# A sketched attention with a squared-ReLU feed-forward on one core: the order of the first weight loads, and the row length of one weight

## The chip, the cores and the metric

One core of a Trainium2 chip runs the whole kernel. The metric is the device time of one execution in microseconds, the median of several. The core's engines work side by side, each through its own queue of instructions in order: TensorE (PE, with the weight loads shown as PEld), VectorE (DVE), ScalarE (ACT), GpSimd (POOL) and SyncE (SP), which here issues nearly all DMA transfers.

## What is computed

Four batches with four heads, 1,088 positions and a head width of 32. q and k are sketched to 64 features, attention is linear in them, and its output, laid out as 4,352 rows of 128, goes through a feed-forward with a hidden width of 2,048. All data are float32.

```python
def phi(x):
    a = np.einsum('rd,bhsd->bhsr', S1, x)          # r = 8
    b = np.einsum('rd,bhsd->bhsr', S2, x)
    return np.einsum('bhsi,bhsj->bhsij', a, b).reshape(*x.shape[:-1], r * r)
q_p, k_p = (phi(q), phi(k))
kv = np.einsum('bhsf,bhsd->bhfd', k_p, v)
z = np.sum(k_p, axis=2)
num = np.einsum('bhsf,bhfd->bhsd', q_p, kv)
den = np.einsum('bhsf,bhf->bhs', q_p, z)[..., None] + 1e-06
x = (num / den).transpose(0, 2, 1, 3).reshape(4352, 128)
h = np.maximum(x @ w_in, 0.0)                      # w_in 128 x 2048
out = h * h @ w_out                                # w_out 2048 x 128
```

## The kernel before

The attention output is kept transposed in SBUF as `xT` (128 x 4,352). The feed-forward runs over ten blocks of its columns (`FC`: 256, 384, 448, 448, 512 five times, 256). For each block it walks through 16 slices of 128 hidden units: `ffn1` (L582) multiplies a slice of `w_in` with the block into PSUM tile `pg`, `relu` (L591, on ACT) takes it to `gt`, `square` (L599 on ACT or L601 on DVE) to `g`, and `ffn2` (L620) adds `w_o` slice times `g` to the output tile `po`. Slices are grouped into units of up to 512 columns: in the first block, unit 0 and 1 hold one slice each and units 2 to 8 two each. PE runs the first products of up to four units ahead of the second products.

Start-up is written out by hand. SP issues its loads in one list: k and the first 256 columns of q for batch 0, eight loads of v, then the ten loads that the change permutes: four quarters of `w_in`, four of `w_o`, and the second and third part of q. `load_wi` (L204) brings a quarter of 512 columns, 128 rows of 2,048 bytes, into `w_in32`. `load_wo` (L209) brings 512 rows of `w_out`; partition p receives the four rows 4p to 4p + 3 of the quarter, which lie together in memory as 2,048 bytes. Hidden unit 4p + j of a quarter thus sits in partition p of slice j. To match this, `cast_wi` (L664, on POOL) rounds a quarter of `w_in32` to the matmul's float32r type and gathers every fourth column, so that slice j holds the hidden units 4i + j.

The first 256 columns of `xT` come from a special short path that ends at L810. What follows in each engine's queue is fixed in advance by a list scheduler (`_Order`), which works with constant estimates of the durations; the engines then wait for one another through semaphores. Around the change these steps stand in this order:

- POOL: the four casts, then 16 small copies (L496) that spread the reciprocal of the denominator (`rc`) into `rd`.
- DVE: `xT` (L810); two transposes of q's second part into `qT` (L288); the squares of units 0 and 1 (L601); `qt` (L468); `pd` (L474), a product of two SBUF operands; a sum (L484) and the reciprocal `rc` (L488); the shuffles `qb`, `qa` (L505) and products `qp` (L520); `bc` (L545), which waits for POOL's copies; and `xT` for the next 384 columns (L552); then the transposes of the next k (L276).
- PE: `ffn1` of units 0, 1 and 2; the sketch of q's second part, `qc` (L295); then `ffn1` and `ffn2` in turn; `nd` (L535), which needs `qp`; `ffn1` of unit 8; and `ffn1` of the second block, which needs the `xT` of L552.

Unit 3 is the first to read the second quarter of the weights, unit 5 the third, unit 7 the fourth. After the ten loads SP issues k, v and q of batch 1, and then output stores (L634) and the loads of later batches as their buffers come free. Each DMA also waits, on SP, for the landing of the one eight places before it.

Of the kernel before, what the change touches and what calls it, by code (L numbers as in the profile page):

```python
# [14 lines left out]
def _ap(t: bass.AP, p0: int, np_: int, off: int, free):  # L15
    p = list(t.ap)[0]
    return bass.AP(
        t.tensor, t.offset + p0 * p[0] + off, [[p[0], np_]] + [list(d) for d in free]
    )
# [85 lines left out]
def kernel(  # L105
# [11 lines left out]
    nc = tc.nc  # L117
# [38 lines left out]
    def sb(name, cols, dt=F32, rows=128):  # L156
        return cpool.tile([rows, cols], dt, tag=name, name=name)
# [9 lines left out]
    w_in32, w_o, w_in = sb("w_in32", 2048), sb("w_o", 2048), sb("w_in", 2048, F32R)  # L167
# [14 lines left out]
    def load_q(eng, b, c0, c1):  # L182
        eng.dma_start(  # L183
            qn[b % 2][:, c0:c1],
            bass.AP(q.tensor, q.offset + b * H * S * D + c0, [[G * D, 128], [1, c1 - c0]]),
        )
# [16 lines left out]
    def load_wi(eng, c):  # L203
        eng.dma_start(  # L204
            w_in32[:, 512 * c : 512 * c + 512], moe_w_in[:, 512 * c : 512 * c + 512]
        )

    def load_wo(eng, c):
        eng.dma_start(  # L209
            w_o[:, 512 * c : 512 * c + 512],  # L210
            bass.AP(
                moe_w_out.tensor, moe_w_out.offset + c * 512 * 128, [[512, 128], [1, 512]]
            ),
        )

# [446 lines left out]

    def cast_wi(c):
        nc.gpsimd.tensor_copy(  # L664
            _ap(w_in, 0, 128, 512 * c, [[128, 4], [1, 128]]),
            _ap(w_in32, 0, 128, 512 * c, [[1, 4], [4, 128]]),
        )

    def keep_warm(n, cols=512):
# [15 lines left out]
        )  # L685
    nc.scalar.copy(ss[:, :], sp[:, 0:80])
    load_wi(nc.sync, 0)
    load_wo(nc.sync, 0)
    load_q(nc.sync, 0, 256, 640)
    for c in range(1, 4):  # L690
        load_wi(nc.sync, c)
        load_wo(nc.sync, c)
    load_q(nc.sync, 0, 640, S)
    keep_warm(W1)
# [76 lines left out]
    for c in range(4):  # L771
        cast_wi(c)
# [308 lines left out]
```

## Time and profile before

| | us |
|---|---|
| median of 3 runs (lowest, highest) | 187.6 (186.36, 187.63) |
| the profiled execution's own time | 187.6 |
| its span, from the first to the last instruction | 185.5 |

The span leaves out 2.1 us around the program. The page gives the busy time of each engine, 40 slices of the span with the busy tenths of each engine, the chain of work that ended last (followed back from the last instruction to whatever released it), and groups of equal instructions. Three rows of the 40 slices:

```profile
PE   8988899999999999999999999999999999999992
...
POOL 4446504418400000770000003830000000000000
...
DMA  4789900100028700000591100002103000300111
```

A slice is 4.6 us; 9 means 90% or more. The DMA row is the mean busy share of the core's 16 DMA engines. The loads concerned and their landing, from issue, as medians of each kind:

```profile
w_in<-in_moe_w_in_dram SPq DMA_DIRECT2D x4, 256.0 KB, 4.8
w_o<-in_moe_w_out_dram SPq DMA_DIRECT2D x4, 256.0 KB, 4.9
```

### The profile page before, as it was taken

The page shows a single profiled execution, that of the slowest core. Times are in us where ns is not written, and L with a number is a line of the kernel's source. Part 1 is how long each engine was busy: PE and PEld are TensorE (multiplying, and loading weights), DVE is VectorE, ACT ScalarE, POOL GpSimd, SP SyncE. Part 2 cuts the span into 40 slices and gives each one's busy share as a digit, 9 for nine tenths or more (in the row PEclk, how much of TensorE's full clock was granted, in tenths as well). Part 3 has the DMA queues.
Part 4 walks back from the last instruction along what each step waited for, and adds up shares of the span by engine and source line. Part 5 has one row for each costly group of instructions (what it writes and reads, how often), then busy time and mean ns, then how long its engine had stood idle before and what let it go on. Part 6 is the DMA issues. An engine that isn't in the chain of part 4 may idle for free.

```text
span 185.5 us, 3893 instructions
## 1 busy us (share of the span) xinstructions
PE 179.4 (97%) x1478; PEld 103.6 (56%) x1478; DVE 120.7 (65%) x254; ACT 135.3 (73%) x262; POOL 37.3 (20%) x157
## 2 busy tenths in 40 slices
PE   8988899999999999999999999999999999999992
PEld 2746666666555556554554545554555555555792
DVE  4969869977993688699527983998243334222420
ACT  3339777769968878599585975795788878777760
POOL 4446504418400000770000003830000000000000
PEclk9999999999999999999999999999999999999999
DMA  4789900100028700000591100002103000300111
GB/s 159 188 277 329 230 5 2 31 1 4 0 44 231 181 0 4 0 0 1 102 310 31 28 0 5 0 0 38 24 0 57 0 0 5 55 0 0 30 27 28
DMA packets 23138, 11.25 MB, mean 61 GB/s; under 512 B 18001, under 2 KB 21073, under 8 KB 23121
## 3 DMA queue, kind: packets, MB, share of 16 engines
q1 hardware_dynamic: 22912, 10.95, 24.1%
q8 instruction: 11, 0.18, 0.5%
q10 hardware_dynamic: 208, 0.07, 0.2%
q14 instruction: 7, 0.05, 0.1%
HBM read 8.78 MB, written 2.23 MB: 59 GB/s over the span
## 4 chain that ended last, share of the span: by engine, by line
PE 86%; SPq 5%; DMA 3%; POOL 2%; issue 1%; DVE 0%
PE po L620 58%; PE pg L582 17%; PE nd L535 3%; DMA w_in<-in_moe_w_in_dram 3%; PE kvp L401 2%; PE pol L615 2%; PE po L615 2%; SPq L195 2%; POOL rd L496 2%; SPq L204 2%; PE qc L295 1%; PE kc L337 1%; SPq L209 1%; POOL w_in L664 1%; SPq L183 0%
## 5 line engine op out<-in xcount | busy, mean ns | idle before, releaser
L620 PE MATMUL po<-g,w_o 128*128 128x512 f32 (+3 forms) x288 | 123.8, 548 | 0.0
L591 ACT ACTIVATE gt<-pg 128x512 f32<-128x512 f32 (+3 forms) x145 | 75.5, 568 | 34.9 <-PE pg L582 34.4
L620 PEld LDWEIGHTS po<-g,w_o 128*128 128x128 f32 x288 | 53.0, 189 | 32.4 <-issue 23.9
L582 PE MATMUL pg<-xT,w_in 128*128 128x512 f32 (+3 forms) x160 | 69.3, 516 | 1.8 <-DVE xT L552 0.6
L599 ACT ACTIVATE g<-gt 128x512 f32<-128x512 f32 (+2 forms) x105 | 60.0, 602 | 1.4
L601 DVE TENSOR_TENSOR g<-gt 128x512 f32<-128x512 f32 (+3 forms) x40 | 27.2, 681 | 40.8 <-ACT gt L591 40.2
L582 PEld LDWEIGHTS pg<-xT,w_in 128*128 128x128 f32 x160 | 28.9, 190 | 31.1 <-ACT gt L591 11.1
L442 POOL COPY kv<-kvt 32x64 f32<-32x64 f32 x48 | 12.1, 252 | 64.4 <-DVE kvt L419 62.3
L496 POOL COPY rd<-rc 32x9 f32<-32x9 f32 (+2 forms) x80 | 16.2, 203 | 11.7 <-DVE rc L488 8.3
L505 DVE STREAM_SHUFFLE qa<-qc 128x576 f32<-128x576 f32 (+2 forms) x20 | 11.6, 652 | 0.0
L520 DVE TENSOR_TENSOR qp<-qa,qb 128x576 f32<-128x576 f32 (+2 forms) x20 | 10.8, 606 | 0.0
L354 DVE TENSOR_TENSOR kp<-fs 128x576 f32<-128x576 f32 x12 | 8.4, 753 | 0.1
L468 DVE STREAM_TRANSPOSE qt<-qc 128x576 f32<-128x576 f32 (+2 forms) x10 | 5.8, 613 | 3.9 <-PE qc L295 3.9
L624 DVE STREAM_TRANSPOSE oT<-po 128x512 f32<-128x512 f32 (+3 forms) x9 | 5.9, 652 | 2.4 <-PE po L620 2.4
L535 PE MATMUL nd<-qp,kv 32*32 32x288 f32 (+2 forms) x320 | 6.8, 353 | 0.0
L545 DVE STREAM_TRANSPOSE bc<-rd 128x576 f32<-128x576 f32 (+2 forms) x10 | 5.8, 606 | 1.0 <-POOL rd L496 0.8
L552 DVE TENSOR_TENSOR xT<-nd,bc 128x576 fp32r<-128x576 f32 (+2 forms) x10 | 5.6, 600 | 1.0 <-PE nd L535 1.0
L505 DVE STREAM_SHUFFLE qb<-qc 128x576 f32<-128x576 f32 (+2 forms) x10 | 6.0, 650 | 0.0
L288 DVE STREAM_TRANSPOSE qT<-qn 128x192 f32<-128x192 f32 (+3 forms) x11 | 5.9, 564 | 0.0
L535 PEld LDWEIGHTS nd<-qp,kv 32*32 32x32 f32 x320 | 3.8, 103 | 3.7 <-issue 2.2
L664 POOL CAST w_in<-w_in 128x512 fp32r<-128x512 f32 x4 | 4.5, 1116 | 6.2 <-DMA w_in<-in_moe_w_in_dram 6.2
L615 PE MATMUL pol<-w_o,g 128*128 128x128 f32 x32 | 5.7, 275 | 0.0
(92 smaller groups left out, 91.5 us busy)
## 6 DMA issues: line engine op xcount, KB each, us to landing
kn<-in_k_dram SPq DMA_DIRECT2D x3, 544.0 KB, 5.3
qn<-in_q_dram SPq DMA_DIRECT2D x3, 544.0 KB, 6.1
vn<-in_v_dram SPq DMA_DIRECT2D x9, 144.0 KB, 4.4
w_in<-in_moe_w_in_dram SPq DMA_DIRECT2D x4, 256.0 KB, 4.8
w_o<-in_moe_w_out_dram SPq DMA_DIRECT2D x4, 256.0 KB, 4.9
out_dram<-oT SPq DMA_DIRECT2D x12, 64.0 KB, 2.0
out_dram<-oT SPq DMA_DIRECT2D x8, 56.0 KB, 2.2
out_dram<-oT SPq DMA_DIRECT2D x8, 48.0 KB, 1.8
```

What stands on the lines that cost most here:

```text
L354: nc.vector.tensor_tensor(out=_ap(st[b, "kp"], 0, 128, 64 * NT * h, [[64, NT], [8, 8], [1, 8]]), in0=_ap(fs, 0, 128, o, [[32, NT], [1, 8], ...
L442: nc.gpsimd.tensor_copy(_ap(st[b, "kv"], 32 * c, 32, 64 * h, [[32, E], [1, 32]]), _ap(st["kvt"], 32 * h, 32, 0, [[64, E], [1, 32]]),)
L496: nc.gpsimd.tensor_copy(st[b, "rd", i0][32 * h : 32 * h + 32, n * c : n * c + n], st["rc"][32 * c : 32 * c + 32, n * h : n * h + n],)
L505: nc.vector.stream_shuffle(in_=banks(st[b, "qc", i0], 2 * x, 0, m), out=_ap(st[b, which, i0], 0, 128, 2 * m * x, [[m, 2], [1, m]]), mask=m ...
L520: nc.vector.tensor_tensor(out=st[b, "qp", i0, e][:, r], in0=st[b, f"qa{e}", i0][:, r], in1=st[b, "qb", i0][:, r], op=mult,)
L535: nc.tensor.matmul(nd[32 * h : 32 * h + 32, 512 * c : 512 * c + m], kv[r, o : o + 32], qp[r, m * h : m * h + m], start=(e == 0), stop=(e = ...
L582: nc.tensor.matmul(st["pg", u][:, n * i : n * i + n], w_in[:, 128 * (d0 + i) : 128 * (d0 + i) + 128], xT[:, c0 : c0 + n],)
L591: nc.scalar.activation(gt[:, 0:w], st["pg", u][:, 0:w], Relu)
L599: nc.scalar.activation(g2[:, 0:w], gt[:, 0:w], Square)
L601: nc.vector.tensor_tensor(out=g2[:, 0:w], in0=gt[:, 0:w], in1=gt[:, 0:w], op=mult)
L615: nc.tensor.matmul(po[x // 128][:, 0:128], g[:, x : x + 128], w, start=(d == 0), stop=(d == NB - 1),)
L620: nc.tensor.matmul(po[0][:, 0:n], w, g, start=(d == 0), stop=(d == NB - 1))
```

## The change

The ten loads behind v are issued in another order. `w_o` is loaded so that partition p receives rows p, 128 + p, 256 + p and 384 + p of a quarter, four rows of 512 bytes; slice j then holds the hidden units 128j to 128j + 127 of the quarter. With that, `cast_wi` copies a quarter's columns in their own order, source and destination without a stride. The sum over the hidden units is taken in another order; nothing else of the computation changes.

| place | before | after |
|---|---|---|
| 1 | w_in quarter 0 | w_in quarter 0 |
| 2 | w_o quarter 0 | w_in quarter 1 |
| 3 | q, columns 256 to 640 | w_o quarter 0 |
| 4 | w_in quarter 1 | q, columns 256 to 640 |
| 5 | w_o quarter 1 | w_in quarter 2 |
| 6 | w_in quarter 2 | w_in quarter 3 |
| 7 | w_o quarter 2 | w_o quarter 1 |
| 8 | w_in quarter 3 | w_o quarter 2 |
| 9 | w_o quarter 3 | w_o quarter 3 |
| 10 | q, columns 640 to 1,088 | q, columns 640 to 1,088 |

```diff
     def load_wo(eng, c):
         eng.dma_start(
-            w_o[:, 512 * c : 512 * c + 512],
+            _ap(w_o, 0, 128, 512 * c, [[128, 4], [1, 128]]),
             bass.AP(
-                moe_w_out.tensor, moe_w_out.offset + c * 512 * 128, [[512, 128], [1, 512]]
+                moe_w_out.tensor, moe_w_out.offset + c * 512 * 128,
+                [[128, 128], [128 * 128, 4], [1, 128]],
             ),
         )
...
     def cast_wi(c):
         nc.gpsimd.tensor_copy(
-            _ap(w_in, 0, 128, 512 * c, [[128, 4], [1, 128]]),
-            _ap(w_in32, 0, 128, 512 * c, [[1, 4], [4, 128]]),
+            w_in[:, 512 * c : 512 * c + 512], w_in32[:, 512 * c : 512 * c + 512]
         )
...
     load_wi(nc.sync, 0)
+    load_wi(nc.sync, 1)
     load_wo(nc.sync, 0)
     load_q(nc.sync, 0, 256, 640)
+    load_wi(nc.sync, 2)
+    load_wi(nc.sync, 3)
     for c in range(1, 4):
-        load_wi(nc.sync, c)
         load_wo(nc.sync, c)
     load_q(nc.sync, 0, 640, S)
```

## The prediction

> **What bounds the kernel now.** I read the page first. PE is busy 97% of the span at full clock, and the chain that ended last is 86% PE, so from the moment PE runs without gaps the end moves only with PE's start-up.
>
> ```profile
> span 185.5 us, 3893 instructions
> ...
> PE 179.4 (97%) x1478; PEld 103.6 (56%) x1478; DVE 120.7 (65%) x254; ACT 135.3 (73%) x262; POOL 37.3 (20%) x157
> ...
> PE 86%; SPq 5%; DMA 3%; POOL 2%; issue 1%; DVE 0%
> ```
>
> The same chain over the first 45 us (start, length, what) shows where start-up ends. The last w_in quarter, issued at 11.30, lands at 16.71; its cast follows; behind the cast POOL's 16 small copies (L496) run to 21.64; then xT, and PE's first matmul of the second column block at 22.71. From there the chain is PE alone.
>
> ```profile
> 11.30 5.41 DMA w_in<-in_moe_w_in_dram
> 16.71 0.05 issue
> 16.77 1.13 POOL w_in L664
> 17.89 0.13 POOL rd L496
> ...
> 21.98 0.59 DVE xT L552 x2
> 22.57 0.14 issue
> 22.71 0.41 PE pg L582
> ```
>
> Last the timeline from 9 to 25 us (start, length, engine, line; in brackets the idle time before and its end):
>
> ```profile
> 7.73 2.09 SPq L204 DMA_DIRECT2D w_in<-in_moe_w_in_dram  x1
> ...
> 12.51 0.63 DVE L288 STREAM_TRANSPOSE qT<-qn 128x192 f32<-128x192 f32 x2
> ...
> 13.16 1.11 POOL L664 CAST w_in<-w_in 128x512 fp32r<-128x512 f32 x1 [1.14 <-DMA w_in<-in_moe_w_in_dram]
> ...
> 13.55 1.34 DVE L601 TENSOR_TENSOR g<-gt 128x256 f32<-128x256 f32 x2 [0.41 <-ACT gt L591]
> ...
> 15.20 1.11 POOL L664 CAST w_in<-w_in 128x512 fp32r<-128x512 f32 x1 [0.92 <-DMA w_in<-in_moe_w_in_dram]
> ...
> 15.48 0.95 DVE L474 TENSOR_TENSOR pd<-qt 128x96 f32<-128x96 f32 x1
> ```
>
> Three things stand in it. First, SP needs 0.43 us for a load, but 2.09 for the second w_in quarter. In that time the instruction queue q8 moves one 16 KB packet (7.58 to 9.68 in the trace's packet records); at 55.25 and 89.10 such packets also coincide with long SP issues (1.62 and 1.77 us). Second, two DVE products with both inputs in SBUF stretch while a cast runs on POOL: the first square takes 1.00 us against 0.41 for its twin, `pd` 0.95 against 0.29 for the larger 128x128 one (L474 at 28.99); both end 0.12 to 0.28 us after the cast. Third, ACT, from 13.68 on, is idle only 0.13, 0.29, 0.51 and 0.60 us up to its relu at 23.16, gaps of 0.03 left out: 1.53 us is the most that earlier weights can give there.
>
> **The change, part by part.** No instruction is added or removed; the orders on PE, DVE, ACT and POOL stay, SP's ten loads behind v are permuted.
>
> *Places.* The ten loads land at 10.85, 11.47, 11.99, 13.11, 13.74, 15.14, 15.76, 16.71, 17.42 and 18.00 in order of issue; I give each place's time to the load that now holds it. w_in's quarters move from places 1, 4, 6, 8 to 1, 2, 5, 6: the second lands at 11.47 (was 13.11), the third at 13.74 (15.14), the fourth at 15.14 (16.71). q's second part moves from 3 to 4, w_o's quarters from 2, 5, 7, 9 to 3, 7, 8, 9. The fetch on q8 begins at 7.58 by a clock that this part of the program does not move, so the hold falls on place 4 again, now q: 13.11 instead of 11.99. That is the change's cost. The load is smaller than the one that held the place (192 KB against 256), so 12.3 is its early end; 13.7 its late one, if place 5 is its row.
>
> *w_o in 512-byte rows.* 512 packets a quarter instead of 128. The packet records give medians of 84 ns for 2,048 B and 27 for 512 B (v's first loads): 32 x 27 = 864 ns per engine instead of 8 x 84 = 672, 0.19 us more per quarter. Bounds: 21 ns would cost nothing; under load 2,048 B packets averaged 105, 1.25 times their median, so 34 ns and 0.41 us. I take 0.19, v's own row. One quarter stands ahead of q, and the smaller q load gives that back. The Trainium skill (DMA: Bandwidth & Descriptors, Why small descriptors are slow) puts about three cycles of overhead on a packet; worked out as an estimate, 4 x 19 / 67 cycles is 13% more, against 29% by the rows here, and the sum would differ by 0.1 us. The three other quarters are first needed by PE at 17.81, 21.10 and 24.00; they land by about 16.2, 17.3 and 18.2 with three times 0.19 added, so they stay hidden by 0.7 us or more even if PE comes to them 0.9 earlier. q's last part, read by DVE at 20.18, and the second k, read at 22.49 and landed at 20.45, shift by at most 0.8 and stay hidden. SP issues 512-row stores in 0.33 to 0.51 us (L634 at 100), near its 0.43 for a load; nothing but loads queues behind it until the store at 34.38.
>
> *Casts without stride.* Four of 1.11 us now. Copies of 16 and 128 columns take 0.20 and 0.29; in a line that makes 0.58 for 512, the lower end; 1.11 is the upper. I take 0.8, between them. The Trainium skill (GPSIMD Engine Reference, Performance pitfalls for Q7 kernels) says that a read step over 8 bytes costs 2.9 cycles an element instead of 1.9; the stride taken away is 16 bytes, and 1.11 x 1.9 / 2.9 would be an estimate of 0.73, which would move the sum by less than 0.1. No row here reads 512 columns unstrided.
>
> *The path.* Up to xT at 12.60 nothing moves. qT starts with q at 13.17 and ends at 13.80 (was 13.14), 0.25 past the first square's start of 13.55. The third cast, 13.80 to 14.60, meets the squares: whichever goes first, the second ends near 15.35 (was 14.89). Then qt to 15.95, and `pd` is free at 15.95, when the fourth cast (15.20 to 16.00) ends: about 0.25 us instead of 0.95. The reciprocal rc ends at 16.83 instead of 17.06. On DVE that is 0.23 us earlier for qp, thus for PE's `nd` (19.64, was 19.87) and the matmuls behind it: 2.10 us from nd's start to the end of issue before the second block (21.10 + 4 x 0.22), so PE is there at 21.74. POOL, whose casts are over, starts its copies at 16.87 instead of 17.84, ends them 3.80 us later at 20.67, and xT is done 0.93 later (21.64 to 22.57 now), at 21.60. PE's wait for xT (0.58) is gone and its matmul comes at 21.8 instead of 22.71: 0.9 us. ACT, given back its 0.60 and 0.23 of the gaps before, follows by 0.83; what is late next is ACT. I take 0.9.
>
> **Sum.** Profiled execution: span 185.5, own time 187.6, 2.1 us around it; the median of the three runs is the same 187.6 (186.36 to 187.63). 185.5 - 0.9 + 2.1 = **186.7 us**.
>
> **Rivals.** *More than that:* q lands at 12.3 (or the hold misses it), DVE does both squares before the third cast, casts take 0.58. Then `pd` follows qt at 15.0, rc ends near 15.9, and ACT's limit decides: all 1.53 us, 186.1; with the spread of the runs shown, 185.3 to 186.7. For it: the fourth cast no longer covers `pd`. Against it: the third cast falls into the squares.
>
> *Slower: 512-byte rows ahead of q.* The place is DVE, in order: qT waits for q, and behind qT stand the squares, qt, pd, rc, qp, and behind those PE's `nd`. 13.11 gives 0.23 us to `nd`; each 0.1 us later costs 0.1. PE has 0.74 more to lose before 22.71 is passed, so it decides from a landing at 13.11 + 0.23 + 0.74 = 14.1, which needs w_o packets of (672 + 1000) / 32 = 52 ns, 1.9 times v's row. At three times, 81 ns, the quarter takes 1.9 us longer, q lands at 15.0, and the kernel takes 188.5. For it: their reads step 64 KB from row to row, a step that no load in the trace has, and 4,352-byte packets of 18.3 to 21.8 us took some 310 ns against a median of 168. Against it: all rows of that size.
>
> *Nothing:* the time gained in start-up is lost again to ACT before 40 us, where PE is busy without a gap but ACT only 11.6 of 14 us: 187.6. I see no queue that would take it.
>
> **How the numbers follow.** Forecast (186.1 to 187.4) 0.45, more 0.25, slower 0.18, nothing 0.12. Range 185.3 to 188.3: from the low end of "more" to most of the slow case. A measurement of this kernel can tell about 1% from no change, 1.9 us; the forecast's 0.9 lies inside. Faster by over 1% takes two thirds of "more" and a seventh of the forecast, by the spread of the runs: 0.23. Slower by over 1% takes two thirds of the slow case: 0.12. Within: 0.65.
>
> **What would show it.** SP's long issue on q's load and not on w_in; q's landing near 13.1; casts of 0.6 to 0.9 us, the last over by 16; `pd` under 0.4 us; PE's first 384-column matmul at 21.8 and no wait for xT before it. I am wrong if 512-byte packets take over 50 ns, if the hold lies elsewhere, or if PE waits again after 23 us.

## The result, and the profile after

| | before | after |
|---|---|---|
| median of 20 executions, us | 187.5 | 186.6 |
| lowest to highest | 186.36 to 188.63 | 185.91 to 188.22 |
| the profiled execution's own time | 187.6 | 187.0 |
| its span | 185.5 | 185.0 |

The ratio of the times is 0.9957, with a 95% interval from 0.9940 to 0.9975: about 0.8 us less. The page of the kernel after, in the lines that were shown of before:

```profile
span 185.0 us, 3893 instructions
...
PE 180.1 (97%) x1478; PEld 104.4 (56%) x1478; DVE 120.1 (65%) x254; ACT 135.0 (73%) x262; POOL 35.2 (19%) x157
...
PE 97%; DVE 0%; issue 0%
```

The loads (5% SPq, 3% DMA) and POOL (2%) have left the chain that ended last; it is PE from end to end, and a wait of PE that is short does not show in it. The timeline from 7 to 25 us:

```profile
7.76 0.50 SPq L183 DMA_DIRECT2D qn<-in_q_dram  x1
8.31 0.91 SPq L204 DMA_DIRECT2D w_in<-in_moe_w_in_dram  x2
9.26 2.93 SPq L209 DMA_DIRECT2D w_o<-in_moe_w_out_dram  x3
...
13.17 0.42 DVE L812 TENSOR_TENSOR xT<-num,bc 128x256 fp32r<-128x256 f32 x1
...
14.12 1.36 POOL L665 CAST w_in<-w_in 128x512 fp32r<-128x512 f32 x2 [1.15 <-DMA w_in<-in_moe_w_in_dram]
...
14.55 1.21 DVE L602 TENSOR_TENSOR g<-gt 128x256 f32<-128x256 f32 x2 [0.41 <-ACT gt L592]
...
16.35 0.26 DVE L475 TENSOR_TENSOR pd<-qt 128x96 f32<-128x96 f32 x1
...
17.30 3.83 POOL L497 COPY rd<-rc 32x3 f32<-32x3 f32 x16 [1.82 <-DVE rc L489]
...
21.47 0.58 DVE L553 TENSOR_TENSOR xT<-nd,bc 128x192 fp32r<-128x192 f32 x2
...
22.20 0.41 PE L583 MATMUL pg<-xT,w_in 128*128 128x384 f32 x1
```

The last cast is over at 15.48 instead of 17.89. `pd` takes 0.26 us, no longer covered by a cast. POOL now waits for `rc`; before, `rc` was done and the casts kept POOL from it. The copies start 0.54 us sooner, and PE's second block comes at 22.20. The view names no wait for `xT` there any more, but the block still stands 0.15 us behind the end of that `xT` (22.05), as it did before (22.57 to 22.71); how much of the wait is left is worked out below. q was not held on SP. And the first block's `xT` is 1.0 us *later* than in the profile of before (13.17, was 12.17), at a point that the change does not touch. So two profiles that differ by 0.5 us in span differ by -1.5 and +1.0 us within. The whole of the +1.0 lies in one group of early matmuls. Timeline of before:

```profile
5.16 1.21 PE L307 MATMUL kf<-ss,kt 128*32 128x64 f32 x72
```

and of after, the same instructions:

```profile
5.23 2.14 PE L308 MATMUL kf<-ss,kt 128*32 128x64 f32 x72
```

The trace's record of the granted TensorE clock shows full speed from 5.03 us on in the one and from 7.24 in the other.

### The profile page after: what moved, and what is told of

It reads as the page before. It is cut to its first block, busy times and chain, and to the rows that moved or that the text cites. A ratio compares the mean times of both kernels' runs of the same rounds, so it can differ in the third digit from the quotient of the medians.

```text
span 185.0 us, 3893 instructions
## 1 busy us (share of the span) xinstructions
PE 180.1 (97%) x1478; PEld 104.4 (56%) x1478; DVE 120.1 (65%) x254; ACT 135.0 (73%) x262; POOL 35.2 (19%) x157
## 4 chain that ended last, share of the span: by engine, by line
PE 97%; DVE 0%; issue 0%
PE po L621 60%; PE pg L583 18%; PE nd L536 4%; PE warm L672 2%; PE kvp L402 2%; PE pol L616 2%; PE po L616 2%; PE qc L296 2%; PE kvp L384 1%; PE kf L308 1%; PE kc L338 1%; PE x L734 1%; PE num L789 0%; PE den L789 0%; PE den L759 0%; PE x L427 0%
## 5 line engine op out<-in xcount | busy, mean ns | idle before, releaser
L616 PE MATMUL po<-w_o,g 128*128 128x128 f32 x32 | 5.7, 275 | 0.0
```

Of the source, the lines that this page charges most:

```text
L616: nc.tensor.matmul(po[x // 128][:, 0:128], g[:, x : x + 128], w, start=(d == 0), stop=(d == NB - 1),)
```

## The experiments

The first question was whether that late clock belongs to the change, the second which part of the change carries the gain. Each kernel below was timed in 10 to 12 executions beside the kernel before on the same chip; ratios are to it, with their 95% interval.

**Both kernels once more**, without an edit.

> The kernel before unaltered, for a second profile. Theory C: its clock may rise early or late too. If late, xT of the first block comes at about 13.6 us, but the w_in landings, which hang on SP, move less, so that the stretch from there to the second block's first matmul shrinks from 10.1 to between 9.0 and 9.8 us. Time 187.5 within 0.4 us, ratio to itself 1.000 within 0.003.

> The changed kernel unaltered, for a second profile. Theory C: the profile of after had PE's matmuls of L307/L308 run 2.07 us instead of 1.21 because the granted clock rose 2.2 us later (7.2 instead of 5.0 us from the span's start), by chance of the execution; the first xT block came 1.0 us later for that, and the gain behind it was 1.5 us, not 0.9. If it is chance, this profile may show either state, and with the early clock a span of 184.0 to 184.4 and the held SP issue on q's second part. If the change causes it, this profile shows the late clock again.

> The changed kernel unaltered, beside the three others on the same chip: 186.6 us within 0.4. If chance moves the clock's rise and the instruction fetch, this profile shows yet another pair of times for them (seen so far: rise at 4.2 to 7.2 us, fetch at 7.6 to 9.3), and the held SP load is again another one than q's second part or the same by chance.

Measured: before again 187.54 us, 1.0008 [0.9989, 1.0027]; after again 186.57, 0.9967 [0.9940, 0.9993]; a third time 186.72, 0.9961 [0.9940, 0.9982]. The effect holds. The clock rose at 4.87 us in this profile of before and at 5.84 and 7.05 in the two of after; in the other kernels of this section it rose between 3.89 and 7.23, with the same early instructions. The stretches between two changes of the clock, in all 14 profiles, last 3.41, 10.24, 167.25, 177.49 or 180.91 us, whole multiples of 3.413, and the 14 rises lie within 3.35 us. A clock that can change only at ticks 3.41 us apart, with the start of the program falling anywhere between two of them, would give this, so the late rise is most likely chance. Of the eight profiles with the new order and the new casts, six rose at 5.84 or later, of the six others one. casts_twice and long_rows rose early with them and rows_casts_only late without the order, so the change neither forces a late rise nor is needed for one; that it makes one no likelier is not shown. The kernel before was not caught with a late rise, so its expected shorter stretch was not seen.

The second profile of before shows the two-input products blocked in another way than the first (its timeline):

```profile
12.86 2.39 POOL L664 CAST w_in<-w_in 128x512 fp32r<-128x512 f32 x2 [1.73 <-DMA w_in<-in_moe_w_in_dram]
...
13.73 1.80 DVE L601 TENSOR_TENSOR g<-gt 128x256 f32<-128x256 f32 x2 [0.41 <-ACT gt L591]
...
17.61 3.83 POOL L496 COPY rd<-rc 32x3 f32<-32x3 f32 x16 [0.81 <-DVE rc L488]
```

Two casts back to back, 1.11 and 1.13 us, hold the two squares for 1.80 us instead of 0.76 (two such that no cast holds up, in after_third), and it is `rc` that comes late, not the last cast: the copies start at 17.61, in the first profile at 17.84.

The held load was not q's second part. In the second profile of after, SP's timeline has

```profile
7.75 0.50 SPq L183 DMA_DIRECT2D qn<-in_q_dram  x1
8.29 2.68 SPq L204 DMA_DIRECT2D w_in<-in_moe_w_in_dram  x2
```

and the 16 KB packet of the instruction queue runs from 8.59 to 10.60. Over all profiles that packet starts between 7.37 and 9.65 us, and the load that SP issues then or next is held until 0.1 to 0.4 us after its end (in rows_casts_only the hold is spread over three loads).

**Each half of the change alone.** The order alone keeps before's rows and casts; rows and casts alone keep before's order. Both were measured on two chips.

```diff
 order_only, order_only_2 (against before)
     load_wi(nc.sync, 0)
+    load_wi(nc.sync, 1)
     load_wo(nc.sync, 0)
     load_q(nc.sync, 0, 256, 640)
+    load_wi(nc.sync, 2)
+    load_wi(nc.sync, 3)
     for c in range(1, 4):
-        load_wi(nc.sync, c)
         load_wo(nc.sync, c)
 rows_casts_only, rows_casts_2 (against after): the same lines back
```

> The ten loads in the new order, w_o still in 2,048-byte rows and the casts still strided (1.11 us each). Theory A, the earlier landings of w_in give the gain (the casts leave POOL and the products of DVE sooner): most of the measured 0.8 to 0.9 us is here, 0.5 to 0.9 us faster than before, and POOL's copies L496 start before 17.5 us counted with xT of the first block at 12.6. Rival B, the shorter casts give it: 0.1 to 0.3 us faster, and pd is still stretched by a cast.

> The order alone once more (the first profile of it had the granted clock at half from 14.5 to 17.9 us). Theory F: the copies start between 17.0 and 17.5 us, since the strided casts still stretch g or pd by 0.5 to 1.4 us; 0.2 to 0.6 us faster than before. Rival A, the order carries the gain: 0.8 us faster, copies at 16.9 or earlier.

> The ten loads in the old order, w_o in 512-byte rows and the casts without stride (0.61 us each in the profile of after). Theory A: 0 to 0.3 us faster than before, since the last w_in quarter still holds the eighth place and lands 0.5 us later behind three w_o quarters of shorter rows. Rival B: 0.5 to 0.9 us faster.

> Rows and casts alone once more. Theory F: the last cast, behind the eighth load, ends near 16.8 to 17.4 and still meets pd or g; copies start between 17.2 and 17.7 us; 0.2 to 0.6 us faster than before. Rival B, the casts carry the gain: 0.8 us faster, copies at 16.9 or earlier.

Measured: the order alone 187.46 us, 0.9978 [0.9947, 1.0009], and 187.30, 0.9981 [0.9956, 1.0006]; rows and casts alone 186.76, 0.9979 [0.9955, 1.0003], and 187.22, 0.9981 [0.9952, 1.0009]. Each half lands near 0.4 us faster both times, about half of the whole, but each interval touches 1.000. These times lie between theory A and rival B, and their intervals exclude neither; that neither half carries all of the gain is likely, not shown. Theory F of the second pair (0.2 to 0.6 us) fits the times, but not the copies: they came at 16.19 and 16.79, where 17.0 to 17.5 and 17.2 to 17.7 were expected. The single profiles can't decide it: they range more than the halves differ. One of the order alone has the copies at 17.64, and the clock halved in passing (the view of busy time by stretches: length, busy time of PE, PEld, DVE, ACT and POOL with counts, then granted clock, DMA share, GB/s):

```profile
14.50:17.80 3.30, 3.30 (x38) 2.66 (x26) 3.13 (x11) 2.17 (x5) 2.49 (x3) 0.50 0.97 360
```

The other has them at 16.19, the earliest of all, in an execution of 185.78 us that was the fastest of its twelve.

**What ends start-up.** Set beside one another, the profiles show a simple rule. POOL's sixteen copies start when both `rc` and the last cast are done (adjoining instructions overlap by up to 0.08 us in these records). PE's second block begins 4.9 us after their start, or 8.36 us after the end of the first `xT`, whichever is later. From there to the end it is 162.8 to 163.2 us in every kernel.

| profile | clock rise | fetch | first xT | rc | last cast | copies | second block | xT to block | copies to block | rest |
|---|---|---|---|---|---|---|---|---|---|---|
| before | 5.03 | 7.58 | 12.60 | 17.06 | 17.89 | 17.84 | 22.71 | 10.11 | 4.87 | 162.8 |
| before_again | 4.87 | 9.21 | 12.78 | 17.54 | 16.80 | 17.61 | 22.50 | 9.72 | 4.90 | 162.8 |
| after | 7.24 | 9.34 | 13.59 | 17.24 | 15.48 | 17.30 | 22.20 | 8.61 | 4.90 | 162.8 |
| after_again | 5.84 | 8.59 | 12.93 | 16.54 | 15.54 | 16.61 | 21.50 | 8.57 | 4.90 | 163.0 |
| after_third | 7.05 | 8.51 | 13.50 | 16.70 | 15.69 | 16.76 | 21.86 | 8.36 | 5.09 | 162.9 |
| order_only | 4.22 | 8.54 | 12.51 | 17.57 | 16.82 | 17.64 | 23.05 | 10.54 | 5.41 | 162.9 |
| order_only_2 | 4.49 | 7.37 | 12.46 | 15.91 | 16.27 | 16.19 | 21.11 | 8.65 | 4.91 | 162.8 |
| rows_casts_only | 7.20 | 9.04 | 13.58 | 17.55 | 16.81 | 17.61 | 22.51 | 8.93 | 4.90 | 162.8 |
| rows_casts_2 | 3.89 | 8.88 | 12.60 | 15.80 | 16.84 | 16.79 | 21.69 | 9.09 | 4.91 | 162.8 |
| casts_twice | 4.48 | 7.38 | 12.49 | 16.11 | 16.90 | 16.85 | 21.75 | 9.26 | 4.90 | 162.8 |
| split_casts | 7.11 | 8.75 | 13.53 | 16.88 | 15.79 | 16.95 | 21.89 | 8.36 | 4.95 | 162.9 |
| long_rows | 5.14 | 7.43 | 12.65 | 15.84 | 16.88 | 16.82 | 21.70 | 9.05 | 4.88 | 163.2 |
| copies_more | 7.23 | 9.61 | 13.59 | 16.90 | 15.89 | 16.96 | 22.75 | 9.16 | 5.79 | 162.8 |
| w_in_first | 6.70 | 9.65 | 13.34 | 16.54 | 14.19 | 16.61 | 21.70 | 8.36 | 5.09 | 162.9 |

(Starts of the clock's rise, the fetch packet, the copies and the block; ends of the others.) The rule gives the start of the block within 0.05 us in 13 of the 14 (copies_more with its longer copies, below). The exception is order_only, where PE's first product waited for a late first cast and the clock fell. Where PE waits for nothing (after_third, split_casts, w_in_first), the block begins 0.67 to 0.68 us behind the start of the four `ffn2` before it. By that mark the copies made PE wait 0.94 and 0.78 us in the two profiles of before, and in two of after still 0.25 and 0.21 us; in after_third, as in split_casts and w_in_first, PE is the later one, and the chain through its start-up has no wait for POOL:

```profile
13.08 0.43 DVE xT L812
...
13.65 0.71 PE pg L583 x4
14.36 0.38 PE qc L296 x29
14.73 0.11 issue
...
16.42 0.06 issue
...
20.02 0.89 PE nd L536 x51
...
22.21 0.18 PE pg L583
```

The copies start at 17.73 on the mean of the two profiles of before and at 16.89 of the three of after, 0.84 us sooner; the second block, 0.75 us sooner. Both are near the measured 0.8; with two and three profiles that range over 0.2 and 0.7 us, that is in part luck. To test the rule and not only read it, the copies were made longer:

```diff
 copies_more (against after)
-        for h in range(H):
+        for h in [h for h in range(H) for _ in range(2 if (b, i0, c) == (0, 8, 0) else 1)]:
             nc.gpsimd.tensor_copy(
                 st[b, "rd", i0][32 * h : 32 * h + 32, n * c : n * c + n],
```

> The changed kernel with the first four of POOL's sixteen copies behind rc (L497) issued twice, same data. Theory F: in nine of ten profiles PE's second block starts 4.9 us behind the first of these copies (4.87 to 4.94; 5.1 in after_third), and the copies start 0.06 us behind rc or behind the last cast, whichever is later; the rest of the span is 162.8 to 163.2. Then four more copies (0.22 us each, with waits up to 0.3) come straight into the time: second block 0.7 to 1.2 us later behind the first copy (5.6 to 6.1), time 0.6 to 1.2 us more than the changed kernel. Rival: PE or ACT sets that point and the copies only happen to end beside it: 0.3 us or less.

Measured: 187.66 us, 1.0007 [0.9985, 1.0029]. The changed kernel was not beside it on that chip; by the ratios to before, 0.9957 to 0.9967 there, copies_more is 0.75 to 0.95 us slower. Its timeline:

```profile
16.96 4.72 POOL L497 COPY rd<-rc 32x3 f32<-32x3 f32 x20 [1.08 <-DVE rc L489]
...
22.02 0.58 DVE L553 TENSOR_TENSOR xT<-nd,bc 128x192 fp32r<-128x192 f32 x2
...
22.75 0.41 PE L583 MATMUL pg<-xT,w_in 128*128 128x384 f32 x1 [0.45 <-ACT g L600]
```

Four copies of 0.22 us lengthen the group from 3.83 to 4.72 us, and the second block stands 5.79 us behind the first copy instead of 4.90, again 0.15 us behind the end of `xT` (22.60). The view puts PE's wait down to ACT's `g`, which ended at the same time; in the profile of after the block begins at 22.20, before that `g` ends at 22.74, so the block does not need it. The first `xT` ends at 13.59 in both profiles, so PE alone would have come at 21.95. The copies, made longer, are the path: 0.89 us put there came out as 0.75 to 0.95 us of time and used up the gain of the change. They are not the only limit of the changed kernel: without them PE would have come 0.25 us sooner at most in its three profiles.

**More and smaller casts.**

```diff
 casts_twice (against after)
-        nc.gpsimd.tensor_copy(
-            w_in[:, 512 * c : 512 * c + 512], w_in32[:, 512 * c : 512 * c + 512]
-        )
+        for _ in range(2 if c > 1 else 1):
+            nc.gpsimd.tensor_copy(
+                w_in[:, 512 * c : 512 * c + 512], w_in32[:, 512 * c : 512 * c + 512]
+            )
 split_casts (against after)
-        nc.gpsimd.tensor_copy(
-            w_in[:, 512 * c : 512 * c + 512], w_in32[:, 512 * c : 512 * c + 512]
-        )
+        for o in range(512 * c, 512 * c + 512, 128):
+            nc.gpsimd.tensor_copy(w_in[:, o : o + 128], w_in32[:, o : o + 128])
```

> The changed kernel with the casts of w_in's third and fourth quarter each issued twice (same data, same result). Theory D: start-up ends with the reciprocal rc (in all six profiles so far PE's second block starts 4.9 to 5.0 us behind its end or the end of the last cast, and the rest of the span is 162.8 to 163.0 us), and the casts act on it by holding up DVE's products with two SBUF inputs. Then 1.2 us more of casts stretch g and pd by 0.6 to 1.2 us and the kernel is that much slower than the changed one. Rival E: casts act through the slices of w_in that PE waits for. Then nothing is lost, since unit 5 reads its slice over 1 us after its cast in the profile of after: within 0.2 us.

> The changed kernel with each cast in four pieces of 128 columns (0.15 to 0.3 us each, 0.6 to 1.1 in all). Theory D: a product waits at most for one piece, so the second g takes 0.45 to 0.7 us instead of 0.83 and rc ends 0.1 to 0.4 us sooner behind the first xT; time 0.1 to 0.4 us less than the changed kernel. Rival E: no gain, and up to 0.2 us lost if the pieces add up to more than one cast.

Measured: casts twice 187.01 us, 0.9978 [0.9955, 1.0001], beside 186.72 and 0.9961 of the changed kernel on that chip: 0.3 us more, where 0.6 to 1.2 was expected, and the intervals overlap. The timeline shows why it is less:

```profile
13.91 1.45 POOL L666 CAST w_in<-w_in 128x512 fp32r<-128x512 f32 x2 [2.49 <-DMA w_in<-in_moe_w_in_dram]
...
14.91 0.56 DVE L475 TENSOR_TENSOR pd<-qt 128x96 f32<-128x96 f32 x1
...
16.85 3.83 POOL L497 COPY rd<-rc 32x3 f32<-32x3 f32 x16
```

The clock rose early and the fetch held an early load here: the squares (13.50 to 14.22) were nearly over when the first of the four casts began, and only `pd` was stretched, by 0.3 us. The second cost fell on POOL's own queue: `rc` was done at 16.11, the last cast at 16.90, and the copies waited for it. Split casts: 186.71 us, 0.9958 [0.9929, 0.9986], no gain to be told from the changed kernel. In its profile the second square took 0.50 us, as expected; the pieces took 0.29 us each, or 0.48 beside a square, so a quarter lasted 1.0 to 1.4 us instead of 0.61.

**Rows of w_o, and another order.** In long_rows `load_wo` is before's, with one contiguous run of 2,048 bytes for each partition; the same work, with another output. In w_in_first the list of loads is changed again:

```diff
 w_in_first (against after)
     load_wi(nc.sync, 1)
-    load_wo(nc.sync, 0)
     load_q(nc.sync, 0, 256, 640)
     load_wi(nc.sync, 2)
     load_wi(nc.sync, 3)
-    for c in range(1, 4):
+    for c in range(4):
         load_wo(nc.sync, c)
```

> The changed kernel with w_o loaded in 2,048-byte rows as before; the rows of w_o then no longer belong to the slices of w_in that they meet, so the output differs from the reference; the amount of work is the same. If 512-byte rows cost what their packets say (0.19 us a quarter, one quarter ahead of q, all hidden), the time is that of the changed kernel within 0.2 us. If they cost on the path, it is 0.4 us or more faster.

> The changed kernel with w_o's first quarter moved behind all of w_in and q's second part (order: two quarters of w_in, q, the two others, w_o). Theory F: the last cast ends 0.5 to 0.9 us earlier, which helps only executions in which it, not rc, starts the copies; 0 to 0.4 us faster than the changed kernel. Rival: w_o's first quarter lands near 15 us, PE's first second product (14.7 to 15.3 us so far) waits for it and passes the wait to ACT: 0 to 0.5 us slower.

Measured: long rows 186.86 us, 0.9966 [0.9941, 0.9992], the changed kernel's time (0.9961 on that chip) within the 0.6 us that the two intervals can tell apart. The 512-byte packets of `w_o` in the profile of after had a median of 27 ns, as forecast. In the profile of long rows the copies waited 1 us for the last cast (16.88, `rc` 15.84): the fetch came at 7.43 and held `w_o` at place 3 for 2.32 us, with both last quarters of `w_in` behind it. w_in first: 186.72 us, 0.9945 [0.9923, 0.9967]. Its casts were over at 14.19 and met no product, but `rc` (16.54) then set the copies, and PE came 5.09 us behind them, by its own queue: 8.36 us behind the first `xT`, without a wait for the copies. It was not set beside the changed kernel on one chip, and that it beats it is not shown.

## Why the prediction was right, point by point

The time (186.7, measured 186.6) and the mechanism held: POOL's copies come free sooner, and PE's wait for the second block's `xT` shrinks to 0.25 us or nothing. The term of 0.9 us measured 0.84 as the mean start of the copies, 0.75 as that of the block, and 0.8 by the ratio. That the single times hit so closely is partly luck, as the first point shows.

- *The path.* Forecast `rc` 16.83, copies 16.87, second block 21.8; the three profiles of after have means of 16.83, 16.89 and 21.85, each with a range of 0.7 us. Two errors cancel in these: the first `xT` ended at 13.34 on the mean, not at 12.60, with the clock rising late, and from there `rc` took 3.49 us, not 4.23. The whole difference lies in the two squares: they ended 1.72 to 2.17 us behind the first `xT`, not 2.75, and from their end to `rc` it was 1.48 us, as forecast. The longer copies of copies_more show that the copies can set the time, as forecast.
- *The casts.* Taken at 0.8 us, measured 0.61, with 0.58 as the forecast's lower end. The Trainium skill's rule (GPSIMD Engine Reference, Performance pitfalls for Q7 kernels) had given an estimate of 0.73; its step from 2.9 to 1.9 cycles is a factor of 1.53, the measured one is 1.82.
- *pd and the squares.* `pd` at 0.26 (0.25 forecast). The second square met a cast in two of three profiles (0.83 instead of 0.42), as forecast.
- *512-byte rows.* Hidden, as forecast, as far as 0.6 us can be told: long_rows takes the same time. The slower rival needed 52 ns for a packet; they took 27.
- *The hold on q.* Wrong. The step said that the fetch begins at 7.58 by a clock that this part of the program does not move, so that place 4 is held. The fetch moves by 2.3 us from execution to execution, and the held load in the three profiles of after was at place 7, 6 and 6. The prediction had named a hold elsewhere as a sign of being wrong; this step was, and the gain did not hang on it. The forecast charged the hold with 0.25 us at the first square. In the three profiles that square begins 0.96 to 0.97 us behind the first `xT`, as before (0.95): q was covered by the 0.41 us in which DVE waits for the first relu. That charge is one part of the 0.6 to 1.0 us by which the squares ended closer behind `xT` than forecast.
- *"Up to xT at 12.60 nothing moves."* The instructions do not; the clock does. The first `xT` ended between 12.46 and 13.59 over the profiles.
- *ACT next.* Wrong. When the copies come early (after_third, split_casts, w_in_first), what is late next is PE's own queue from the first `xT` on, and so the first `xT` itself, which a late clock moves. `nd` is no cause there: DVE's last `qp` ends at 19.44 in after_third and PE is busy until `nd` begins. ACT's gap before unit 8's relu, 0.36 us, waits for PE.

Open: how the gain is divided between order and casts, and what the change gives when the clock rises as early as in the two profiles of before, which no profile of the changed kernel caught.

## What to carry to other kernels

When a kernel is one dense engine after a short start-up, look for the instruction whose start plus a constant gives the end, check it across several profiles, and lengthen it by a known amount before you trust it. Then look for the second one close behind it: it limits what a further gain on the first can give. A cast that runs on GpSimd has two prices, the queue behind it there and the two-input SBUF products of VectorE beside it; both are paid by where it falls, so shorten it and let it fall before them. Differences of half a microsecond between two single profiles are not evidence: compare distances from a mark inside each.

## What the runs showed of the hardware

- The granted TensorE clock reached full speed at any time from 3.9 to 7.2 us after the span's start with the same instructions; a late rise slowed 72 short matmuls from 1.21 to 2.14 us. The first `xT` ended at 12.46 to 12.78 us with rises up to 5.14 and at 13.50 to 13.59 with rises from 7.05. Once it fell to half for 3.4 us in the middle. All stretches between two changes were whole multiples of 3.413 us (1, 3, 49, 52 and 53 of them).
- One 16 KB packet of the instruction queue, 0.9 to 2.1 us long, came with a hold of the DMA that SP issued then or next, until 0.1 to 0.4 us after the packet's end, in every profile. The Trainium skill (Runtime: NRT & Kernel Launch, Instruction fetch mechanics) calls such block crossings mostly hidden; here one adds 0.7 to 1.9 us to a load's issue where SP has loads to issue (in one profile, spread over three loads).
- A GpSimd cast and a VectorE product with two SBUF inputs hold each other up, both ways: `g` went from 0.41 to 1.00 us beside a strided cast, and in the three profiles of after casts of 0.61 us took 0.77 to 0.87 when a product was running.
